# Attention in fp32: sums of values in 64-row by 32-column tiles over two halves of the keys, with a new order of the matmuls

## The chip, the cores and the metric

One Trainium2 chip, one core. The metric is the time of one execution on the device in microseconds (us); shorter is better.

## What is computed

Two rounds of the same two layers on x of 2048 rows and 640 columns, all in fp32:

```python
x = x + _A_ref(_layernorm(x), A_wqkv, A_wo)              # attention, 32 heads of 20
x = x + _B_ref(_layernorm(x), B_w1, B_b1, B_w2, B_b2)    # 640 -> 1536, squared relu, -> 640
# and both lines once more

scores = jnp.einsum("bhqd,bhkd->bhqk", q, k) * (Dh ** -0.5)
p = _softmax(scores, axis=-1)
o = jnp.einsum("bhqk,bhkd->bhqd", p, v)
```

## The kernel before

A layer A runs in three stages: the projections to q, k and v (`qkv`), the attention (`attention`), and the product with wo. Then comes layer B. The change lies in `attention`.

**Blocks and tiles.** Four heads form a group, and 512 queries of a group form a block `t`; there are 32 blocks. A block goes through the 2048 keys in 16 tiles of 128 keys, so a layer has 512 key tiles. For one key tile TensorE does three things:

- *Scores* (`score`, line 565): four matmuls, one for each head, with keys as rows of the result. q and k are laid out so that a head uses 62 rows of the array: two heads (letter `a` in the order below) lie on rows 0 to 63, the other two (`b`) on rows 64 to 127. A score on the lower half of the rows can so run beside one on the upper half. ScalarE takes the exponential of each result (line 572) and writes it to a tile `e`.
- *Sums of values* (`pv`, line 577): four matmuls, one for each head, which multiply `e` by the values (with a column of ones, for the sum of the weights) and add to one bank over the 16 key tiles of the block. Each uses all 128 rows and 32 columns of the array. The letter `V` stands for the four. They are plain fp32, and each shows as two passes in the trace.
- *Maxima* for a later block (`smax`, line 481, letters `m` on the lower half of the rows and `n` on the upper): the softmax needs the largest score of each query beforehand, so scores are computed a second time with queries as rows, and VectorE reduces each result to its maximum (line 493). A part of this work was done already in `qkv`. 

**PSUM banks.** The scores go through banks 0 to 3 in turn (`ps_st`), the maxima through banks 4, 5 and 6 (`sm_ring`), and the sums of values of a block collect in bank 7. When a block's 16 tiles are through, `finish` copies bank 7 out on VectorE (line 590), and small steps on POOL and SyncE's DMA queue divide by the sum of the weights.

**Order.** Nothing is scheduled automatically here: instructions stand on each engine in the order in which the program makes them. In `attention` this order is written by hand in the strings `ORDERS`. Each string covers 8 key tiles, and its key is the number of pairs of maxima in it. `pairs()` chooses among them by how many maxima are still due; it chooses 12 nearly all the time. TensorE takes its instructions in this order, and one that has to wait for a bank holds back those behind it. The last 16 key tiles of a layer run in another way (`both_heads`, line 1091, two scores for one exponential at line 1098), and have no maxima left.

Of the kernel before, what the change touches and what calls it, by code (L numbers as in the profile page):

```python
# [25 lines left out]
NQB = S // QB  # L26
NG = H // 4
NKT = S // P
# [11 lines left out]
def tile_layers(  # L40
# [11 lines left out]
    nc = tc.nc  # L52
# [10 lines left out]
    def name(p):  # L63
        n_alloc[0] += 1
        return f"{p}{n_alloc[0]}"

    def slot(shape, dtype, label):
        return arena.tile(shape, dtype, tag="slot", name=name(label))

    def dma(eng, dst, src):  # L70

        if dst.dtype == F32R:
            dst = dst.bitcast(F32)
        if src.dtype == F32R:
            src = src.bitcast(F32)
        eng.dma_start(dst, src)
# [4 lines left out]
    banks = psum.tile([P, 8, 512], F32, tag="banks", name="banks")  # L81
# [172 lines left out]
    def split_to(dst_hi, dst_lo, src):  # L254

        nc.scalar.copy(dst_hi, src)
        nc.vector.tensor_sub(dst_lo, src, dst_hi.bitcast(F32))  # L257
# [12 lines left out]
    def pool_hi(dst, src):  # L270
        nc.gpsimd.tensor_copy(dst, src)  # L271
# [3 lines left out]
    def pool_lo(dst, a, b):  # L275
        m = nc.gpsimd.tensor_sub(dst, a, b)
        if last_row:
            after(m, last_row.pop(), "VectorE and Pool share a port")
# [144 lines left out]
    k_t, q_t, v_t, mx_t, kept = {}, {}, {}, {}, {}  # L423
    left, done, split = {}, set(), {}
# [26 lines left out]
    def load_q(t):  # L451
        g, qb = divmod(t, NQB)
        q_t[t] = slot([P, 2, QB], F32R, "q")
        rows_of_heads(q_t[t], d_qk[0, qb], g)
# [34 lines left out]
    def smax(ring, t, p, sub, c, par):  # L489

        dst = ring("sm")
        by_queries(dst, t, p, sub, c, par)
        nc.vector.tensor_reduce(  # L493
            maxima(t)[:, 2 * par + p, sub, c : c + 1], dst, axis=AX.X, op=ALU.max
        )
# [75 lines left out]
        )  # L571
        nc.scalar.activation(es[p][:, par, :], dst, AF.Exp, scale=SCALE)  # L572

    def pv(acc, t, kt, es, heads=(3, 2, 1, 0)):
        for h in heads:
            p, par = divmod(h, 2)
            nc.tensor.matmul(  # L577
                acc[32 * h : 32 * h + 32, :],
                v_t[t // NQB, kt // 8][:, kt % 8, 32 * h : 32 * h + 32],
                es[p][:, par, :],  # L580
                start=(kt == 0),
                stop=(kt == NKT - 1),
            )

    def finish(t, acc):


        g, qb = divmod(t, NQB)
        o = slot([P, 2, QB], F32, "o")
        nc.vector.tensor_copy(o[:, 0, :], acc)  # L590
        res = []

        def store(q):
            ot = res.pop().rearrange("p l t -> p (l t)")
            for h in range(4):
                r0 = (4 * g + h) * DH
                dma(q, d_o[r0 : r0 + DH, qb], ot[32 * h : 32 * h + DH])

        if t == NBLK - 1:

            def invert():
                dst = ps_all("rs")
                nc.tensor.matmul(dst, sums_t, o[:, 0, :], start=True, stop=True)
                nc.vector.reciprocal(o[:, 1, :], dst)

            def divide():
                nc.vector.tensor_mul(o[:, 0, :], o[:, 0, :], o[:, 1, :])
                res.append(slot([P, 2, QB], F32R, "ot"))
                split_to(res[0][:, 0, :], res[0][:, 1, :], o[:, 0, :])

            return [invert, divide, lambda: store(nc.scalar)]

        few = small.tile([P, 16], F32, tag="few", bufs=2, name=name("few"))
        for h in range(4):
            dma(nc.sync, d_s[t, h : h + 1], o[32 * h + DH : 32 * h + DH + 1, 0, :])

        def load():
            dma(nc.sync, few, d_s[t].rearrange("h (q j) -> (h q) j", j=16))

        def invert():  # L620
            nc.gpsimd.tensor_tensor(few, few, minus_t, op=ALU.pow)  # L621

        def spread():
            dma(nc.sync, d_r[t].rearrange("h (q j) -> (h q) j", j=16), few)

        def gather():
            for h in range(4):
                dma(nc.sync, o[32 * h : 32 * h + 32, 1, :], d_r[t, h].partition_broadcast(32))

        def divide():  # L630
            ot = slot([P, 2, QB], F32R, "ot")
            nc.gpsimd.tensor_mul(o[:, 0, :], o[:, 0, :], o[:, 1, :])
            pool_hi(ot[:, 0, :], o[:, 0, :])
            pool_lo(ot[:, 1, :], o[:, 0, :], ot[:, 0, :].bitcast(F32))
            res.append(ot)

        return [load, invert, spread, gather, divide, lambda: store(nc.sync)]
# [46 lines left out]
    def qkv(first, x_src, rest, scores):  # L684
# [271 lines left out]


    ORDERS = {
        16: "bananVanmbanmbbmannaVbmnambVbamnmbVm" * 2,
        15: "anbmnanbaabmbnammbnaVbmbmmbVmbananVanmbanVnambmbVanbmnaVnmbaanVmbbanmV",  # L960
        14: "mbbbanmbbmambmVanannaVmbnaaanVbmabnmVanbmbmbVnaanmbVmabmbanVbmannaVn",
        13: "baanmbVmbanambbnbmVanbmnaVnaabnmbVanbmaanVnmbbanaVmnbmabVabbmmnaVm",
        12: "naambbmVanmbambVbmannabVnabnmabVabnmbanVbbmnanaVbmmbaanVbmbmnaaV",
    }

    def attention(first, x_src, first_rows):
        last = NBLK * NKT
        es_of = {}
        e_n.clear()
        weights.extend(slot([P, 2, QB], F32, "e") for _ in range(6))  # L970
        st_n, sm_n = [0, 0], [0, 0]
        state = {"begun": -1, "done": 0, "acc": None, "debt": 0}
        sm_ring = Ring(4, 5, 6)
        todo = [
            (t, p, sub, c)
            for t in range(NBLK)
# [11 lines left out]
        ends = {x[0]: n for n, x in enumerate(todo)}  # L988
# [3 lines left out]
        rows = {"next": min(t for t in range(NBLK) if t not in done), "at": None}  # L992
# [33 lines left out]
        def op(o):  # L1026
            if o in "ab":
                par = "ab".index(o)
                i, p = divmod(st_n[par], 2)
                if i >= last:  # L1030
                    return
                st_n[par] += 1
                if i > state["begun"]:
                    state["begun"] = i
                    begin(i)
                score(i // NKT, i % NKT, 2 * p + par, es_of.setdefault(i, {}))
            elif o in "mn":
                par = "mn".index(o)
                n = sm_n[par]
                if n == len(todo):  # L1040
                    return
                t, p, sub, c = todo[n]
                if n == firsts[t] and par == 0:
                    for s in blocks[blocks.index(t) :][:2]:
                        if s not in q_t:
                            load_q(s)
                if (t // NQB, c) not in k_t or t not in q_t:
                    return
                sm_n[par] += 1
                smax(sm_ring, t, p, sub, c, par)  # L1050
                if n == ends[t] and min(sm_n) > n:
                    over.add(t)
                    if t * NKT > state["begun"] + 2 * NKT:
                        del q_t[t]
            else:
                i = state["done"]
                if i >= last or i < last - NKT and min(st_n) < 2 * (i + 1):
                    return
                t, u = divmod(i, NKT)
                if u == 0:  # L1060
                    state["acc"] = banks[:, 7, :]
                pv(state["acc"], t, u, es_of.pop(i))
                state["done"] += 1
                if u == NKT - 1:
                    steps = finish(t, state["acc"])
                    split.update((i + j, f) for j, f in zip((4, 6, 7, 9, 11, 12), steps))
                t = rows["next"]
                if rows["at"] is not None:
                    if state["begun"] >= rows["at"]:
                        mrows_load(t)  # L1070
                        rows.update(next=t + 1, at=None)
                elif t in over and t in q_t and state["begun"] >= (t - 2) * NKT + 4:
                    mrows_max(t)
                    mrows(t)
                    rows["at"] = state["begun"] + 2
# [26 lines left out]
        def pairs():  # L1102

            n, i = min(sm_n), state["begun"] + 1
            most = max(
                [8 * (e + 1 - n) / max(t * NKT - 3 - i, 1) for t, e in ends.items() if e >= n],
                default=0,
            )
            state["debt"] += most
            n = min(max(int(state["debt"]), 12), 16)  # L1110
            state["debt"] -= n
            return n

        free.extend((5, 6))
        for o in "abab":
            op(o)
# [14 lines left out]
            both_heads(p)  # L1131
        while state["done"] < last:
            op("V")
            for p in (1, 0):
                if state["wide"] < last:
                    both_heads(p)
# [356 lines left out]
```

## Time and profile before

| | |
|---|---|
| median of 2 runs | 3583.48 us (3583.39 to 3583.57) |
| span of the profiled execution, first to last instruction | 3581.5 us |
| what lies around the span (median less span) | 2.0 us |
| busy: TensorE matmuls | 3569.0 us, 100% |
| busy: VectorE | 2753.5 us, 77% |
| busy: ScalarE | 2647.3 us, 74% |
| TensorE's granted clock | full in all slices |

The profiled execution has no time of its own beside its span; the two timed runs stand for it. In the rows, PE is TensorE's matmuls, PEld its weight loads, DVE is VectorE, ACT ScalarE. A matmul's start is shown with its weight load, also where the array takes up the data only once the weights are in; its end is modelled. Attention fills the stretches from about 310 to 1394 us and from about 2090 to 3174 us.

### The profile page before, as it was taken

The page shows a single profiled execution, that of the slowest core. Times are in us where ns is not written, and L with a number is a line of the kernel's source. Part 1 is how long each engine was busy: PE and PEld are TensorE (multiplying, and loading weights), DVE is VectorE, ACT ScalarE, POOL GpSimd, SP SyncE. Part 2 cuts the span into 40 slices and gives each one's busy share as a digit, 9 for nine tenths or more (in the row PEclk, how much of TensorE's full clock was granted, in tenths as well). Part 3 has the DMA queues.
Part 4 walks back from the last instruction along what each step waited for, and adds up shares of the span by engine and source line. Part 5 has one row for each costly group of instructions (what it writes and reads, how often), then busy time and mean ns, then how long its engine had stood idle before and what let it go on. Part 6 is the DMA issues. An engine that isn't in the chain of part 4 may idle for free.

```text
span 3581.5 us, 67667 instructions
## 1 busy us (share of the span) xinstructions
PE 3569.0 (100%) x25560; PEld 2121.6 (59%) x25560; DVE 2753.5 (77%) x5085; ACT 2647.3 (74%) x5146; POOL 805.2 (22%) x880
## 2 busy tenths in 40 slices
PE   9999999999999999999999999999999999999999
PEld 7896343333334335999988954333334433369998
DVE  8778999999999993455567789999999999824443
ACT  3778999999999995122237789999999999942221
POOL 6531434211211211111153201211211211211110
PEclk9999999999999999999999999999999999999999
DMA  9765555323211136834477652232232211367221
GB/s 305 274 230 167 168 157 155 105 69 81 57 44 51 46 95 204 262 99 115 134 275 244 192 149 70 62 81 60 66 79 54 52 39 45 112 216 248 74 80 39
DMA packets 377397, 452.58 MB, mean 126 GB/s; under 512 B 176642, under 2 KB 223746, under 8 KB 377070
## 3 DMA queue, kind: packets, MB, share of 16 engines
q1 hardware_dynamic: 376254, 445.89, 41.6%
q8 instruction: 201, 3.29, 0.4%
q10 hardware_dynamic: 816, 2.36, 0.2%
q14 instruction: 126, 1.03, 0.1%
HBM read 273.83 MB, written 174.30 MB: 125 GB/s over the span
## 4 chain that ended last, share of the span: by engine, by line
PE 96%; DVE 2%; DMA 1%; issue 0%; ACT 0%; POOL 0%; SPq 0%; ACTq 0%; DVEq 0%
PE banks L577 28%; PE banks L565 20%; PE banks L481 16%; PE banks L293 13%; PE banks L331 10%; PE banks L1259 9%; DVE mx L493 1%; PE banks L1091 1%; DMA q<-d_qk 0%; ACT e L1098 0%; DVE bst L244 0%; DVE xnT L257 0%; DVE x L252 0%; DMA d_qk<-ev 0%; PE banks L408 0%
## 5 line engine op out<-in xcount | busy, mean ns | idle before, releaser
L572 ACT ACTIVATE e<-banks 128x512 f32<-128x512 f32 x3968 | 2049.4, 604 | 61.1 <-PE banks L481 1.7
L493 DVE TENSOR_REDUCE mx<-banks 128x1 f32<-128x512 f32 x3076 | 1929.6, 683 | 208.4 <-PE banks L481 137.2
L481 PE MATMUL banks<-k,q 60*128 60x512 f32 x3586 | 1244.3, 427 | 1.0 <-DMA q<-d_qk 0.5
L565 PE MATMUL banks<-q,k 62*128 62x512 f32 x3968 | 1118.7, 434 | 0.4 <-DVE mx L510 0.4
L577 PE MATMUL banks<-e,vg 128*32 128x512 f32 x8192 | 1091.0, 605 | 1.5 <-ACT e L1098 1.5
L565 PEld LDWEIGHTS banks<-q,k 62*128 62x128 f32 x3968 | 584.4, 185 | 657.8 <-ACT e L572 625.6
L481 PEld LDWEIGHTS banks<-k,q 60*128 60x128 f32 x3586 | 582.0, 184 | 283.1 <-DVE mx L493 210.8
L510 DVE CUSTOM_DVE_ANT_0 rl<-banks,rl 128x512 f32<-128x512 f32 x510 | 332.6, 688 | 101.6 <-PE banks L481 91.0
L331 PE MATMUL banks<-xnT,wqk 64*128 64x512 f32 x2400 | 379.7, 394 | 0.3 <-ACT mark_t L333 0.3
L1244 ACT ACTIVATE r<-banks,b_t 128x512 f32<-128x512 f32 x96 | 66.2, 689 | 419.7 <-PE banks L293 418.3
L577 PEld LDWEIGHTS banks<-e,vg 128*32 128x32 f32 x8192 | 161.1, 108 | 360.2 <-issue 333.1
L502 ACT ACTIVATE rl<-banks 128x512 f32<-128x512 f32 x510 | 270.8, 597 | 98.9 <-PE banks L481 93.6
L1259 PE MATMUL banks<-w,h 128*128 128x320 f32 x2304 | 340.4, 309 | 0.0
L1259 PEld LDWEIGHTS banks<-w,h 128*128 128x128 f32 x2304 | 339.2, 188 | 1.2
L293 PE MATMUL banks<-xnT,w 128*128 128x512 f32 x1440 | 329.4, 389 | 0.0
L331 PEld LDWEIGHTS banks<-xnT,wqk 64*128 64x128 f32 x2400 | 286.4, 185 | 34.3 <-issue 2.4
L293 PEld LDWEIGHTS banks<-xnT,w 128*128 128x128 f32 x1440 | 269.6, 188 | 55.3
L271 POOL CAST mr<-nt 128x32 fp32r<-128x32 f32 x64 | 13.4, 209 | 1143.5 <-DVE nt L536 1143.5
L621 POOL TENSOR_TENSOR few<-few,minus_t 128x16 f32<-128x16 f32 x62 | 179.8, 2900 | 215.6 <-DMA few<-d_s 213.7
L331 PE MATMUL banks<-wv,xnT 64*128 64x320 f32 x1920 | 199.2, 307 | 0.9 <-ACT mark_t L333 0.9
L331 PEld LDWEIGHTS banks<-wv,xnT 64*128 64x128 f32 x1920 | 186.5, 185 | 2.7 <-ACT mark_t L333 1.4
L1245 DVE TENSOR_TENSOR r<-r 128x512 f32<-128x512 f32 x96 | 74.3, 774 | 124.0 <-ACT r L1244 124.0
(86 smaller groups left out, 2010.8 us busy)
## 6 DMA issues: line engine op xcount, KB each, us to landing
q<-d_qk SPq DMA_DIRECT2D x242, 240.0 KB
d_qk<-ev SPq DMA_DIRECT2D x80, 512.0 KB
k<-d_qk SPq DMA_DIRECT2D x152, 240.0 KB
x<-d_x SPq DMA_DIRECT2D x84, 320.0 KB
d_qk<-ev SPq DMA_DIRECT2D x80, 256.0 KB
d_o<-ot SPq DMA_DIRECT2D x248, 80.0 KB
ot<-d_o SPq DMA_DIRECT2D x38, 512.0 KB
d_v<-v SPq DMA_DIRECT2D x32, 512.0 KB
```

The costliest lines, as they stand in the source:

```text
L293: nc.tensor.matmul(dst, a, b, start=(n == 0), stop=(n == last))
L331: m = nc.tensor.matmul(ch["dst"][:, :width], *pair, start=first, stop=last)
L481: nc.tensor.matmul(dst, q_t[t][b : b + 60, p, sub * P : (sub + 1) * P], k_t[t // NQB, c][b : b + 60, p, :], start=True, stop=True,)
L493: nc.vector.tensor_reduce(maxima(t)[:, 2 * par + p, sub, c : c + 1], dst, axis=AX.X, op=ALU.max)
L502: nc.scalar.activation(res, dst, AF.Relu)
L510: nc.vector.tensor_tensor_reduce(out=r, in0=dst, in1=r, scale=1.0, scalar=LEAST, op0=ALU.add, op1=ALU.max, accum_out=maxima(t)[:, 2 * par ...
L565: nc.tensor.matmul(dst, k_t[t // NQB, kt // 4][b : b + 62, p, (kt % 4) * P : (kt % 4 + 1) * P], q_t[t][b : b + 62, p, :], start=True, stop ...
L572: nc.scalar.activation(es[p][:, par, :], dst, AF.Exp, scale=SCALE)
L577: nc.tensor.matmul(acc[32 * h : 32 * h + 32, :], v_t[t // NQB, kt // 8][:, kt % 8, 32 * h : 32 * h + 32], es[p][:, par, :], start=(kt == 0 ...
L621: nc.gpsimd.tensor_tensor(few, few, minus_t, op=ALU.pow)
L1245: nc.vector.tensor_mul(r, r, r)
L1259: nc.tensor.matmul(dst[:, :HALF], hs[f][:, hx, i * P : (i + 1) * P], w_2.piece(at_2(f0 + f, hw, hf)), start=(f == 0 and (hx, hw) == THREE[0]),
```

## The change

The sums of values are taken in two halves of the keys: letter `V` is the four matmuls on rows 0 to 63, letter `W` the four on rows 64 to 127. Each is so a tile of 64 rows and 32 columns. `V` adds to bank 7 and `W` to bank 6, and `finish` adds the two. Bank 6 is no longer there for the maxima, which go through banks 4 and 5 alone. The strings of the order are new, and there are three of them instead of five.

```diff
-    def pv(acc, t, kt, es, heads=(3, 2, 1, 0)):
+    def pv(acc, t, kt, es, half, heads=(3, 2, 1, 0)):
+
+        rows = slice(64 * half, 64 * half + 64)
         for h in heads:
             p, par = divmod(h, 2)
             nc.tensor.matmul(
                 acc[32 * h : 32 * h + 32, :],
-                v_t[t // NQB, kt // 8][:, kt % 8, 32 * h : 32 * h + 32],
-                es[p][:, par, :],
+                v_t[t // NQB, kt // 8][rows, kt % 8, 32 * h : 32 * h + 32],
+                es[p][rows, par, :],
...
-    def finish(t, acc):
+    def finish(t, accs):
...
-        nc.vector.tensor_copy(o[:, 0, :], acc)
+        nc.vector.tensor_copy(o[:, 0, :], accs[0])
+        nc.vector.tensor_add(o[:, 0, :], accs[1], o[:, 0, :])
...
     ORDERS = {
-        16: "bananVanmbanmbbmannaVbmnambVbamnmbVm" * 2,
...
-        12: "naambbmVanmbambVbmannabVnabnmabVabnmbanVbbmnanaVbmmbaanVbmbmnaaV",
+        12: "babnambanVWmbanVWm" * 4,
+        14: "amnabmbnVWanbamnbmVW" * 4,
+        16: "amnabmbnVWanbamnbmVW" * 4,
     }
...
-        sm_ring = Ring(4, 5, 6)
+        halves = [0, 0]
+        accs = [banks[:, 7, :], banks[:, 6, :]]
+        sm_ring = Ring(4, 5)
...
-                [8 * (e + 1 - n) / max(t * NKT - 3 - i, 1) for t, e in ends.items() if e >= n],
+                [8 * (e + 1 - n) / max(t * NKT - 5 - i, 1) for t, e in ends.items() if e >= n],
...
-            n = min(max(int(state["debt"]), 12), 16)
-            state["debt"] -= n
+            n = min(max(int(state["debt"]) & ~1, 12), 16)
+            state["debt"] = max(state["debt"] - n, -1)
...
         while state["done"] < last:
             op("V")
+            op("W")
```

On TensorE, in the middle of the second attention, two key tiles stood as follows before. `L481` is a matmul for a maximum, `L565` one for a score, `L577` two of the sums of values; "waits DVE" is a wait for VectorE to have emptied the bank, "waits Activation" one for ScalarE.

```order
L577 MATMUL banks<-e_4744,vg_5877 32x512 x2
L577 MATMUL banks<-e_4743,vg_5877 32x512 x2
L565 MATMUL banks<-q_6209,k_4881 128x512 [waits Activation_49] x2
L481 MATMUL banks<-k_5325,q_6234 128x512 [waits DVE_49] x2
L565 MATMUL banks<-q_6209,k_4881 128x512 [waits Activation_49] x2
L481 MATMUL banks<-k_5325,q_6234 128x512 [waits DVE_49]
L577 MATMUL banks<-e_4746,vg_5877 32x512 x2
L577 MATMUL banks<-e_4745,vg_5877 32x512 x2
```

Each key tile had its four scores and three maxima between two groups of sums. Now, in the same part of the program (`L579` is the line of the sums of values in the changed kernel):

```order
L579 MATMUL banks<-e_4746,vg_6279 32x512 x2
L579 MATMUL banks<-e_4745,vg_6279 32x512 x2
L481 MATMUL banks<-k_5310,q_5955 128x512 [waits DVE_49]
L565 MATMUL banks<-q_5634,k_4992 128x512 [waits Activation_49] x3
L481 MATMUL banks<-k_5310,q_5955 128x512 [waits DVE_49]
L565 MATMUL banks<-q_5634,k_4992 128x512 [waits Activation_49]
L481 MATMUL banks<-k_5310,q_5955 128x512 [waits DVE_49]
L565 MATMUL banks<-q_5634,k_5092 128x512 [waits Activation_49] x2
L481 MATMUL banks<-k_5310,q_5955 128x512 [waits DVE_49]
L579 MATMUL banks<-e_4748,vg_6279 32x512 x2
L579 MATMUL banks<-e_4747,vg_6279 32x512 x2
```

This is a long stretch of six scores and four maxima (`m`, then `babnamban`); behind it come eight matmuls of sums, `V` and `W`, of which the first four are shown. Then follows a short stretch of two scores and two maxima (`mban`), and again `V` and `W`:

```order
L481 MATMUL banks<-k_5310,q_5955 128x512 [waits DVE_49]
L565 MATMUL banks<-q_5634,k_5092 128x512 [waits Activation_49] x2
L481 MATMUL banks<-k_5310,q_5955 128x512 [waits DVE_49]
L579 MATMUL banks<-e_4744,vg_6279 32x512 x2
L579 MATMUL banks<-e_4743,vg_6279 32x512 x2
```

So two key tiles still hold eight scores and six maxima, but they lie 10 and 4, where before they lay 7 and 7. This unit of two key tiles fills 960 of the 1024 key tiles of the two layers; 32 are the last 16 of each layer, 16 run by the string of 14, and the rest stand at the beginnings and ends. On VectorE, at the end of a block, before:

```order
L493 TENSOR_REDUCE mx_5287<-banks 128x1 [waits PE_49] x27
L590 COPY o_5497<-banks 128x512 [waits DMAHW3_49,PE_49]
L493 TENSOR_REDUCE mx_5287<-banks 128x1 [waits PE_49] x12
L525 TENSOR_REDUCE nm_88<-mx_913 128x16
L536 STREAM_TRANSPOSE nt_5588<-nm_88 128x32 [waits DVE_49,Pool_49]
```

And now:

```order
L493 TENSOR_REDUCE mx_5388<-banks 128x1 [waits PE_49] x26
L592 COPY o_5624<-banks 128x512 [waits DMAHW3_49,PE_49]
L593 TENSOR_TENSOR o_5624<-banks,o_5624 128x512 [waits DVE_49,PE_49]
L493 TENSOR_REDUCE mx_5388<-banks 128x1 [waits PE_49] x10
L525 TENSOR_REDUCE nm_88<-mx_913 128x16
L536 STREAM_TRANSPOSE nt_5716<-nm_88 128x32 [waits DVE_49,Pool_49]
```

The addition of the two banks stands behind the copy, ahead of the reductions of the next long stretch. L525 and L536, which prepare the maxima of a block, stand behind ten reductions instead of twelve, which is behind the last reduction of a long stretch.

More of the change, by code (lines that the diff above doesn't have):

```diff
@@ L958, in tile_layers @@
     ORDERS = {
-        16: "bananVanmbanmbbmannaVbmnambVbamnmbVm" * 2,
-        15: "anbmnanbaabmbnammbnaVbmbmmbVmbananVanmbanVnambmbVanbmnaVnmbaanVmbbanmV",
-        14: "mbbbanmbbmambmVanannaVmbnaaanVbmabnmVanbmbmbVnaanmbVmabmbanVbmannaVn",
-        13: "baanmbVmbanambbnbmVanbmnaVnaabnmbVanbmaanVnmbbanaVmnbmabVabbmmnaVm",
-        12: "naambbmVanmbambVbmannabVnabnmabVabnmbanVbbmnanaVbmmbaanVbmbmnaaV",
+        12: "babnambanVWmbanVWm" * 4,
+        14: "amnabmbnVWanbamnbmVW" * 4,
+        16: "amnabmbnVWanbamnbmVW" * 4,
     }
@@ L971, in attention @@
         st_n, sm_n = [0, 0], [0, 0]
-        state = {"begun": -1, "done": 0, "acc": None, "debt": 0}
-        sm_ring = Ring(4, 5, 6)
+        state = {"begun": -1, "done": 0, "debt": 0}
+        halves = [0, 0]
+        accs = [banks[:, 7, :], banks[:, 6, :]]
+        sm_ring = Ring(4, 5)
         todo = [
@@ L1055, in op @@
             else:
-                i = state["done"]
+                half = "VW".index(o)
+                i = halves[half]
                 if i >= last or i < last - NKT and min(st_n) < 2 * (i + 1):
@@ L1059, in op @@
                 t, u = divmod(i, NKT)
-                if u == 0:
-                    state["acc"] = banks[:, 7, :]
-                pv(state["acc"], t, u, es_of.pop(i))
+                pv(accs[half], t, u, es_of[i], half)
+                halves[half] += 1
+                if min(halves) == state["done"]:
+                    return
                 state["done"] += 1
+                es_of.pop(i)
                 if u == NKT - 1:
-                    steps = finish(t, state["acc"])
+                    steps = finish(t, accs)
                     split.update((i + j, f) for j, f in zip((4, 6, 7, 9, 11, 12), steps))
```

## The prediction

> **What bounds the kernel now.** I read the page first, then the groups of instructions in a steady part of the attention, then single rows. The page:
>
> ```profile
> span 3581.5 us, 67667 instructions
> PE 3569.0 (100%) x25560; PEld 2121.6 (59%) x25560; DVE 2753.5 (77%) x5085; ACT 2647.3 (74%) x5146; POOL 805.2 (22%) x880
> ```
>
> TensorE is never idle, but its ends are modelled, so this does not yet say that it sets the pace. The groups and busy times between 500 and 1200 us:
>
> ```profile
> 500.00:1200.00 700.00, 700.00 (x4945) 278.88 (x4943) 637.85 (x1050) 680.89 (x1319) 166.26 (x175) 1.00 0.30 82
> L572 ACT ACTIVATE e<-banks 128x512 f32<-128x512 f32 x1319 | 681.4, 604 | 19.1
> L493 DVE TENSOR_REDUCE mx<-banks 128x1 f32<-128x512 f32 x989 | 620.6, 683 | 60.3 <-PE banks L481 36.4 <-PE banks L565 22.6
> L577 PE MATMUL banks<-e,vg 128*32 128x512 f32 x2640 | 351.6, 605 | 0.0
> L481 PE MATMUL banks<-k,q 60*128 60x512 f32 x988 | 335.4, 431 | 0.0
> ```
>
> A key tile has eight rows on L577 (four heads, two passes), so 2640 rows are 330 key tiles, **2.12 us each**, with 989 / 330 = 3.0 maxima. ScalarE (681 of 700 us) and VectorE (638) are nearly full too. Which of the three sets the pace, single rows tell (start, length, engine, line):
>
> ```profile
> 801.60 1.07 PE L577 MATMUL banks<-e,vg 128*32 128x512 f32 x8
> 802.05 0.61 PE L577 MATMUL banks<-e,vg 128*32 128x512 f32 x4
> 802.59 0.50 PE L565 MATMUL banks<-q,k 62*128 62x512 f32 x1
> 802.60 0.50 PE L481 MATMUL banks<-k,q 60*128 60x512 f32 x1
> 802.93 0.39 PE L565 MATMUL banks<-q,k 62*128 62x512 f32 x1
> 802.94 0.62 PE L481 MATMUL banks<-k,q 60*128 60x512 f32 x2
> 803.17 0.62 PE L565 MATMUL banks<-q,k 62*128 62x512 f32 x2
> 803.72 1.07 PE L577 MATMUL banks<-e,vg 128*32 128x512 f32 x8
> 809.99 1.57 ACT L572 ACTIVATE e<-banks 128x512 f32<-128x512 f32 x3
> ```
>
> From sums to sums: 803.72 - 801.60 = 2.12. The sums take two passes 0.45 apart (802.05 - 801.60), and 0.99 until the first score. Scores and maxima go in pairs, one on each half of the rows: the second pair 0.34 after the first, later ones 0.23 apart (803.17 after 802.94). Seven matmuls make four on one half: 0.34 + 2 x 0.23 = 0.80 from first to last; then 0.32 to the next sums, which closes the period (0.99 + 0.80 + 0.32 = 2.11). No wait is left in it: **TensorE sets the pace.** ScalarE could go faster: three exponentials back to back take 1.57, the last 0.61, so one every 0.48, or 1.92 for a key tile.
>
> Two costs are in these steps beyond the streaming. A pair takes 0.23, yet 0.32 pass before the sums; and the second pass starts at 802.05, so should be through by 802.50 as the first was after 0.45, yet the first scores load at 802.59 and stream another 0.11 later (0.34 against 0.23). So each change between 64x128 and 128x32 tiles costs about 0.1 of emptying, and exposes the weight load.
>
> **The change, part by part.** *1. Sums in eight tiles.* Is the emptying still there when the tiles are 64 rows high on both sides? No row shows 64x128 against 64x32. The nearest is the end of the attention, where 128x32 sums are followed by the 128x128 product with wo, so that only the columns change:
>
> ```profile
> 1393.25 1.06 PE L577 MATMUL banks<-e,vg 128*32 128x512 f32 x8 [0.74 <-ACT e L1098]
> 1394.24 0.56 PE L293 MATMUL banks<-wo,ot 128*128 128x320 f32 x2
> ```
>
> 0.99 again, the same as where rows and columns both change. I take it that a change of columns alone empties the array, so a group of sums keeps its 0.99 + 0.32. The Trainium skill says so more widely: "TensorEngine Tiling (Array Packing)", Key Properties, has it that any change of the tiling mode, as against another tile of the same mode, drains TensorE. By that rule V and W drain as before and the sum is the one below; without it the third or fourth rival holds.
>
> `V` and `W` lie on different rows and add to different banks. The four tiles of a group run at once now (eight passes of 0.6 in 1.07), and so do a score and a maximum on the two halves (802.59 and 802.60), so I let the eight run at once. The four more starts cost about 0.03 (estimate: the modelled 1.07 holds two passes 0.45 apart and 0.61 long, which leaves about 0.01 for three starts). So 1.02 for `V W`; bounds 0.99 and, if they do not overlap at all, twice that.
>
> *2. The balance of the halves.* Two key tiles now have 10 and 4 matmuls, so 5 and 2 pairs instead of 4 and 4. If nothing waited: 1.03 + 0.34 + 2 x (0.32 + 1.02) = 4.05, or 2.03 for a key tile, 0.09 less than now.
>
> *3. Two banks for maxima.* How long does one use of a bank take?
>
> ```profile
> 808.97 0.29 PEld L481 LDWEIGHTS banks<-k,q 60*128 60x128 f32 x2
> 809.53 0.69 DVE L493 TENSOR_REDUCE mx<-banks 128x1 f32<-128x512 f32 x1 [0.25 <-PE banks L481]
> 551.82 1.94 DVE L493 TENSOR_REDUCE mx<-banks 128x1 f32<-128x512 f32 x3
> 552.55 0.18 PEld L481 LDWEIGHTS banks<-k,q 60*128 60x128 f32 x1
> 552.72 0.39 PE L481 MATMUL banks<-k,q 60*128 60x512 f32 x1
> ```
>
> An idle VectorE begins its reduction 0.56 after the weight load (0.45 after streaming begins). The load at 552.55 waits for the reduction begun at 551.82: 0.73 from a reduction's start to the next use of its bank. That is **1.29 for one use of a bank**. Reductions back to back come every 0.60 to 0.63 (three in 1.94, the last 0.69); I take 0.60. With two banks, the third maximum of a stretch waits for the first, and the fourth for the second. Everything behind a waiting matmul waits too, since TensorE's order is fixed: the scores behind it, the sums, and so ScalarE.
>
> Worked through, with T = 0 at the first weight load of a long stretch, M1 to M4 its maxima, M5 and M6 those of the short one:
> - M1 loads at 0; reduction at 0.56; its bank is free at 1.29.
> - M2 comes third on its half, streams at 0.57 and has data at 1.02, but VectorE is busy until 1.16; bank free at 1.16 + 0.73 = 1.89.
> - M3 could stream at 0.80. It loads at 1.29; reduction at 1.85.
> - M4 loads at 1.89 and streams at 2.00, instead of 1.03 without waits; reduction at 2.45, bank free at 3.18. **The stretch is 0.97 longer.**
> - `V W` load at 2.00 + 0.32 = 2.32 and last until 3.34. VectorE runs dry at 3.05.
> - Short stretch: M5 loads at 3.34 (its bank is free since 1.85 + 0.73 = 2.58), M6 streams at 3.68 (free since 3.18). M5's reduction is at 3.90, M6's at 4.50. No wait.
> - `V W` load at 4.00, until **5.02**. Then M1's bank is free since 4.63, M2's from 5.23, before 5.02 + 0.57.
>
> So 2.51 for a key tile against 2.12: +0.39 x 960 = **+374 us**. ScalarE needs 8 x 0.48 = 3.84 of the 5.02 and VectorE 6 x 0.60 = 3.60, so neither binds. The bounds: 2.03 if no bank is waited for; about 2.57 if `V W` take 0.06 more.
>
> *4. Copy and addition at a block's end.*
>
> ```profile
> 821.97 0.68 DVE L590 COPY o<-banks 128x512 f32<-128x512 f32 x1
> 822.57 3.73 DVE L493 TENSOR_REDUCE mx<-banks 128x1 f32<-128x512 f32 x6
> 826.53 1.89 DVE L493 TENSOR_REDUCE mx<-banks 128x1 f32<-128x512 f32 x3 [0.24 <-PE banks L481]
> L257 DVE TENSOR_TENSOR xnT<-banks,xnT 128x512 fp32r<-128x512 f32 x20 | 12.8, 679 | 5.9 <-ACT xnT L256 5.9
> ```
>
> Now VectorE makes up for the copy by dropping its pauses of a quarter of a microsecond (six reductions in a row), at no cost to TensorE. The addition is priced by a subtraction with one operand in a bank: 0.68 long, 0.60 to 0.68 for what is behind it. Copy and addition begin when `W` ends, at about T = 0.1, so M1's reduction starts at about 1.4 instead of 0.56, and M2, M3, M4 move with it: +0.84, bounds 0 and 0.84. No pause covers it there, as the two banks wait for this very reduction. 60 blocks x 0.84 = +50 us. L525 and L536 (0.21 each) fall into VectorE's pause between 3.05 and 3.90. The sums of the next block come long after the addition.
>
> *5. The rest.* The string of 14 (16 key tiles) has four maxima in each stretch, so each key tile costs about 2.32 + 1.02 = 3.34: +1.2 x 16 = +20 us; some of it comes back as key tiles without maxima, so bounds 0 and 20. The last 16 key tiles of a layer are ScalarE's:
>
> ```profile
> L1098 ACT ACTIVATE e<-banks 128x1024 f32<-128x1024 f32 x24 | 22.2, 1239 | 0.0
> L577 PE MATMUL banks<-e,vg 128*32 128x512 f32 x88 | 11.7, 605 | 0.0
> ```
>
> Eleven key tiles in these 20 us, 1.82 each, with two exponentials of 22.2 / 24 = 0.93. TensorE needs 0.99 + 0.34 + 0.32 = 1.65 of it, so 0.03 more is hidden; without that cover it would be 1 us in all. The DMAs of `finish` are the same and leave about 0.7 later, with steps spread over several key tiles.
>
> Sum: 3581.5 of the profiled execution + 374 + 50 + 20 = 4025.5, and with the 2.0 between span and median about **4027**; I say 4025.
>
> **The rivals.** *First, it works as meant* (2.03): the waits for banks are hidden and the better balance shows: 3583 - 0.09 x 960 = 3497, faster. It needs a bank's use to be under 0.69 (M1 to M3 without waits), about half of the 1.29 in the rows. 5%.
>
> *Second, `W` runs behind `V`.* `pv` issues head by head, two passes for each. Were passes started strictly in this order, the sums would now take five steps of 0.45; they take 0.99, so a later head passes an earlier one. Still, `W`'s first passes could stand behind `V`'s second: +0.45 in each of 976 key tiles, 4025 + 439 = 4464. In the Trainium skill, "TensorE: Matmul & The Clock Gate", Part 3, matmuls keep strict program order in start and end; by that rule this rival holds, and the trace speaks against the rule. 5%.
>
> *Third, no emptying, but the weight loads stay exposed.* Each half goes on by itself. The upper half's round is then b, b, M2 (0.46), M4 a bank's use later (1.75), `W` at 1.98 for 0.88 (0.45 for its first pass, a little less for its last), b, M6, `W` again: 1.98 + 0.88 + 0.46 + 0.88 = 4.20, and 2 x 0.14 for loads: 4.48, or 2.24. +0.12 x 960 + 50 + 20 = 3768. 14%.
>
> *Fourth, not slower: neither emptying nor exposed loads.* The same round without the 0.28 is 2.10 for a key tile; -0.02 x 960 + 50 + 20 = 3634, +1.4%. The bank's use then just eats what the missing emptying gives. It decides if a score on the lower half starts while `W` still runs on the upper. The two identical 0.99 speak against it. 8%.
>
> **How the numbers follow.** The forecast has 68%. Its own range is 3930 to 4110 (`V W` 0.06 longer: +58; steps 4 and 5 at zero: -70). The range is 3700 to 4120: with the third rival, without the first, second and fourth (18%). 2% is about what a measurement of this kernel can tell from no change. Faster by over 2%: the first, 0.05. Within 2%: the fourth, 0.08. Slower: 68 + 5 + 14 = 0.87.
>
> **What would show it.** Groups of sums alternately about 1.7 and 3.3 us apart, so 5.0 for two; 0.32 and 1.02 around `V W`; two waits of L481's load for VectorE in each long stretch; VectorE and ScalarE at about 75 and 80% in the attention. If eight passes take much over 1.1, or scores start under a running `W`, step 1 is wrong; if L481 does not wait, step 3 is.

## Result and profile after

| | before | after |
|---|---|---|
| time, median of 2 runs | 3583.48 us | 4037.36 us (4036.27 to 4038.45) |
| ratio, with 95% interval | | 1.127 [1.125, 1.129] |
| span of the profiled execution | 3581.5 us | 4034.5 us |
| VectorE busy | 77% | 71% |
| ScalarE busy | 74% | 66% |

The change makes the kernel 12.7% slower; 4025 was forecast. The head of the page of the changed kernel, the shares of its chain by engine, and the clock of its 40 slices:

```profile
span 4034.5 us, 84165 instructions
PE 3803.3 (94%) x33752; PEld 2125.6 (53%) x33752; DVE 2850.5 (71%) x5149; ACT 2653.9 (66%) x5146; POOL 804.7 (20%) x880
...
PEclk9999999999999999999999999999999999999999
...
PE 84%; DVE 13%; issue 1%; DMA 1%; ACT 1%; POOL 0%; SPq 0%; DVEq 0%; ACTq 0%; POOLq 0%
```

TensorE has 8192 rows more (33752 against 25560: the sums in eight tiles) and yet, for the first time, idle time. VectorE, which has hardly more work than before, now stands on 13% of the chain. The groups between 500 and 1200 us (busy and mean duration, then idle time before them and what ended it), with the busy times of the stretch (PE, PEld, DVE, ACT, POOL, and the granted clock) ahead of them, and two rows of its waits (total, times, longest) behind:

```profile
500.00:1200.00 700.00, 638.80 (x6184) 229.56 (x6178) 550.16 (x881) 556.27 (x1073) 148.81 (x162) 1.00 0.27 77
```

```profile
L493 DVE TENSOR_REDUCE mx<-banks 128x1 f32<-128x512 f32 x813 | 522.9, 686 | 146.1 <-PE banks L565 108.6 <-PE banks L481 37.4
L481 PE MATMUL banks<-k,q 60*128 60x512 f32 x813 | 356.1, 464 | 61.0 <-DVE mx L493 60.7
L579 PE MATMUL banks<-e,vg 64*32 64x512 f32 x4296 | 294.6, 605 | 0.0
```

```profile
PEld banks L481 <- DVE mx L493: 335.8, 407, 1.8
PEld banks L565 <- ACT e L572: 33.6, 123, 0.8
```

A key tile has sixteen rows of sums now: 4296 / 16 = 268.5 key tiles in the 700 us, 2.61 us each against 2.12. Matmuls of L481 wait 60.7 us for VectorE to empty a bank, and the weight loads of L481 335.8, while VectorE itself is idle for 146.1 us before L493, waiting for TensorE's results. Two engines that wait for each other in turn, neither of them full: this is how too few buffers look. (Of the loads' waits, two in each unit of two key tiles cost nothing: they lie under the sums, the 0.84 in the rows below.) The weight loads of one unit, and its matmuls:

```profile
799.51 0.18 PEld L481 LDWEIGHTS banks<-k,q 60*128 60x128 f32 x1 [0.84 <-DVE mx L493]
...
800.79 0.18 PEld L481 LDWEIGHTS banks<-k,q 60*128 60x128 f32 x1 [0.75 <-DVE mx L493]
801.22 0.18 PEld L565 LDWEIGHTS banks<-q,k 62*128 62x128 f32 x1 [0.17 <-ACT e L572]
801.39 0.18 PEld L481 LDWEIGHTS banks<-k,q 60*128 60x128 f32 x1
...
802.84 0.18 PEld L481 LDWEIGHTS banks<-k,q 60*128 60x128 f32 x1 [0.84 <-DVE mx L493]
```

```profile
799.51 0.50 PE L481 MATMUL banks<-k,q 60*128 60x512 f32 x1
799.52 0.73 PE L565 MATMUL banks<-q,k 62*128 62x512 f32 x3
800.08 0.39 PE L481 MATMUL banks<-k,q 60*128 60x512 f32 x1
800.79 0.49 PE L481 MATMUL banks<-k,q 60*128 60x512 f32 x1 [0.31 <-DVE mx L493]
801.39 0.50 PE L481 MATMUL banks<-k,q 60*128 60x512 f32 x1
801.82 1.09 PE L579 MATMUL banks<-e,vg 64*32 64x512 f32 x16
802.84 0.50 PE L481 MATMUL banks<-k,q 60*128 60x512 f32 x1
803.19 0.40 PE L481 MATMUL banks<-k,q 60*128 60x512 f32 x1
803.51 1.09 PE L579 MATMUL banks<-e,vg 64*32 64x512 f32 x16
804.53 0.50 PE L481 MATMUL banks<-k,q 60*128 60x512 f32 x1
```

With T = 0 at 799.51, the six maxima stand at 0, 0.57, 1.28, 1.88, 3.33 and 3.68, the two groups of sums at 2.31 and 4.00, and the next unit begins at 5.02. The table of the forecast had 0, 0.57, 1.29, 1.89, 3.34 and 3.68, 2.32 and 4.00, 5.02. The third maximum waits 0.75; the fourth shows no wait of its own, since a score ahead of it waits 0.17 for ScalarE (801.22). At the end of a block, VectorE:

```profile
844.42 1.29 DVE L493 TENSOR_REDUCE mx<-banks 128x1 f32<-128x512 f32 x2 [0.76 <-PE banks L565]
845.68 0.69 DVE L592 COPY o<-banks 128x512 f32<-128x512 f32 x1
846.48 0.69 DVE L593 TENSOR_TENSOR o<-banks,o 128x512 f32<-128x512 f32 x1
847.09 2.56 DVE L493 TENSOR_REDUCE mx<-banks 128x1 f32<-128x512 f32 x4
```

and on TensorE the first and the third maximum of the stretch behind it, the third 0.73 after the reduction's start at 847.09:

```profile
845.57 0.50 PE L481 MATMUL banks<-k,q 60*128 60x512 f32 x1
...
847.82 0.50 PE L481 MATMUL banks<-k,q 60*128 60x512 f32 x1 [1.28 <-DVE mx L493]
```

### The profile page after: what moved, and what is told of

It is laid out like the page before. It is cut to its first block, busy times and chain, and to the rows that moved or that the text cites. A ratio compares the mean times of both kernels' runs of the same rounds, so it can differ in the third digit from the quotient of the medians.

```text
span 4034.5 us, 84165 instructions
## 1 busy us (share of the span) xinstructions
PE 3803.3 (94%) x33752; PEld 2125.6 (53%) x33752; DVE 2850.5 (71%) x5149; ACT 2653.9 (66%) x5146; POOL 804.7 (20%) x880
## 4 chain that ended last, share of the span: by engine, by line
PE 84%; DVE 13%; issue 1%; DMA 1%; ACT 1%; POOL 0%; SPq 0%; DVEq 0%; ACTq 0%; POOLq 0%
PE banks L579 24%; PE banks L481 22%; PE banks L293 12%; DVE mx L493 10%; PE banks L331 9%; PE banks L1266 8%; PE banks L565 8%; DVE o L593 1%; DVE o L592 1%; DMA q<-d_qk 0%; PE banks L1097 0%; DVE bst L244 0%; ACT e L1104 0%; SPq L76 0%; ACT e L572 0%
## 5 line engine op out<-in xcount | busy, mean ns | idle before, releaser
L493 DVE TENSOR_REDUCE mx<-banks 128x1 f32<-128x512 f32 x3076 | 1976.3, 686 | 550.3 <-PE banks L565 389.6
L481 PE MATMUL banks<-k,q 60*128 60x512 f32 x3586 | 1531.5, 454 | 216.8 <-DVE mx L493 214.3
L481 PEld LDWEIGHTS banks<-k,q 60*128 60x128 f32 x3586 | 622.5, 184 | 1307.2 <-DVE mx L493 1218.6
L565 PE MATMUL banks<-q,k 62*128 62x512 f32 x3968 | 1277.9, 443 | 3.2 <-ACT e L572 2.8
L579 PE MATMUL banks<-e,vg 64*32 64x512 f32 x16384 | 1120.4, 603 | 1.4 <-ACT e L1104 1.4
L565 PEld LDWEIGHTS banks<-q,k 62*128 62x128 f32 x3968 | 560.5, 185 | 130.9 <-ACT e L572 127.8
L579 PEld LDWEIGHTS banks<-e,vg 64*32 64x32 f32 x16384 | 186.1, 105 | 314.5 <-issue 309.1
L293 PE MATMUL banks<-xnT,w 128*128 128x512 f32 x1440 | 329.4, 389 | 0.0
```

Source lines behind the costliest of these rows:

```text
L293: nc.tensor.matmul(dst, a, b, start=(n == 0), stop=(n == last))
L481: nc.tensor.matmul(dst, q_t[t][b : b + 60, p, sub * P : (sub + 1) * P], k_t[t // NQB, c][b : b + 60, p, :], start=True, stop=True,)
L493: nc.vector.tensor_reduce(maxima(t)[:, 2 * par + p, sub, c : c + 1], dst, axis=AX.X, op=ALU.max)
L565: nc.tensor.matmul(dst, k_t[t // NQB, kt // 4][b : b + 62, p, (kt % 4) * P : (kt % 4 + 1) * P], q_t[t][b : b + 62, p, :], start=True, stop ...
L579: nc.tensor.matmul(acc[32 * h : 32 * h + 32, :], v_t[t // NQB, kt // 8][rows, kt % 8, 32 * h : 32 * h + 32], es[p][rows, par, :], start=(k ...
```

## Experiments

The theory to be tried, which held only in part (the table behind experiment 4): the change costs what it does because two banks do not carry the maxima; the new order and the split of the sums matter little beside that. One rival is that the new order costs the time (10 and 4 matmuls, where ScalarE or VectorE run dry); the other that the split sums do (more starts, or `W` behind `V`). In the diffs, "before" and "after" say from which kernel an experiment departs; "time" is the median, and ratios are to the kernel before (3583.3 to 3584.0 in these comparisons).

**1. Two banks alone** (from before).

```diff
-        sm_ring = Ring(4, 5, 6)
+        sm_ring = Ring(4, 5)
```

> The kernel before with one thing changed: the maxima go through two banks (4, 5) instead of three; sums and order stay. My theory (the third maximum of a stretch waits 1.29 us for the first one's bank): in the old order each key tile has three maxima, so each waits about 0.6, and what stands behind it too: 2.7 to 2.9 us for a key tile instead of 2.12, about 4160 to 4300 us. Rival A (the uneven order of 10 and 4 matmuls is what costs, two banks are enough): 3583. Rival B (the 64-row tiles cost it): 3583.

Time 4332.15 us, 1.209 [1.206, 1.213]: a little above the range given. Rows of its groups between 500 and 1200 us:

```profile
L481 PE MATMUL banks<-k,q 60*128 60x512 f32 x727 | 301.9, 458 | 105.7 <-DVE mx L493 102.2
...
L577 PE MATMUL banks<-e,vg 128*32 128x512 f32 x1936 | 257.8, 605 | 0.0
```

1936 / 8 = 242 key tiles, 2.89 us each, with 102.2 us of idle TensorE before L481 that VectorE ends. Sums and order are untouched here, so the loss of the bank is enough by itself. In the old order it costs more than the whole change does.

**2. The new order alone** (from before: the new strings without `W`, and the two lines that choose among them; three banks for maxima).

```diff
-        12: "naambbmVanmbambVbmannabVnabnmabVabnmbanVbbmnanaVbmmbaanVbmbmnaaV",
+        12: "babnambanVmbanVmbabnambanVmbanVmbabnambanVmbanVmbabnambanVmbanVm",
...
+            n = min(max(int(state["debt"]) & ~1, 12), 16)
```

> The kernel before with the new order alone: 10 and 4 matmuls between the sums, sums still of 128 rows in one bank, three banks for the maxima. If only the banks for maxima matter, M4 alone waits a little (1.40 instead of 1.03): about 2.2 for a key tile, 3660. My theory with the four banks of the scores counted in the same way (the fifth and sixth score of the long stretch wait for the exponentials of the first two, which end 1.18 and 1.65 after the stretch's start): M4 at 1.76, 4.72 for two key tiles, about 3812. Rival A (the order is the whole cost): about 4000. Rival that the better balance shows: about 3500.

Time 3860.62 us, 1.077 [1.074, 1.081]; about 50 more than expected. The order is not free. Between 500 and 1200 us, a row of the groups and two of the waits:

```profile
L577 PE MATMUL banks<-e,vg 128*32 128x512 f32 x2320 | 309.0, 605 | 0.0
```

```profile
PEld banks L481 <- DVE mx L493: 240.3, 289, 0.8
PEld banks L565 <- ACT e L572: 114.5, 290, 0.8
```

2320 / 8 = 290 key tiles, 2.41 us each. The 289 waits of L481, two in a unit, are those under the sums, which cost nothing; three banks are enough for the maxima. But the loads of scores wait for ScalarE twice in a unit, 114.5 / 145 = 0.79 in all:

```profile
801.61 0.18 PEld L565 LDWEIGHTS banks<-q,k 62*128 62x128 f32 x1 [0.46 <-ACT e L572]
802.10 0.18 PEld L565 LDWEIGHTS banks<-q,k 62*128 62x128 f32 x1 [0.31 <-ACT e L572]
```

The fifth and sixth score of a stretch find the four banks of `ps_st` full. Without waits the unit should be 3.99 here (the 4.05 of step 2 of the prediction, less 0.03 for each of two groups of sums that are not split), and 3.99 + 0.77 = 4.76 with them; from the sums of one unit to those of the next the rows have 4.81 (799.39 to 804.20).

**3. The new order with two banks** (experiment 2 and the edit of experiment 1; sums as before). What is then left to the changed kernel is the split sums alone.

> The kernel before with the new order and two banks for the maxima, but the sums as they were (128 rows, one bank, no addition). It differs from the changed kernel only in the sums, so it prices the new tiles alone. My theory: 0.03 for each of about 976 key tiles and 54 us for the additions (the run without them) less than the changed kernel: about 3954. If the 64-row tiles save emptying: 4037 or more. If they cost more than I think: under 3930.

Time 3960.64 us, 1.105 [1.102, 1.109], as expected. With two banks the new order is so 371 us faster than the old (4332.15), with three 277 us slower. The changed kernel's time less this one is 77 us: the price of the split sums. Against experiment 2 the loss of the third bank costs only 100 us here (3960.64 less 3860.62).

**4. The split sums and two banks in the old order** (from after).

```diff
-        12: "babnambanVWmbanVWm" * 4,
+        12: "naambbmVWanmbambVWbmannabVWnabnmabVWabnmbanVWbbmnanaVWbmmbaanVWbmbmnaaVW",
```

> The changed kernel with the old strings, V written as VW: two accumulators, 64-row tiles, two banks for maxima, seven matmuls in each stretch. My theory: as the kernel before with two banks, and 0.03 for the eight tiles and about 50 us for the additions: 4240 to 4380, slower than with the new order. Rival A (the uneven order is the cost): back to about 3600 to 3660. Rival B (the 64-row tiles are the cost): about 4000.

In this kernel and in the second one of experiment 7, the string of 14, which runs 8 key tiles of a layer, lets the scores run so far ahead that two heads' exponentials of a key tile are written over before they are summed; the sums of these key tiles are not the right ones, but the instructions are the same. Time 4420.3 us, 1.234 [1.230, 1.237], above the range again. Against experiment 1 it is 88 us, so the split sums cost much the same here as in the new order (77). Order and banks by themselves, and with the split sums below them, in us:

| | old order | new order |
|---|---|---|
| three banks for maxima | 3583 (before) | 3861 |
| two banks for maxima | 4332 | 3961 |
| two banks and split sums | 4420 | 4037 (the change) |

The bank costs 749 in the old order and 100 in the new one; the new order costs 277 with three banks and wins 371 with two. So the 454 us of the change cannot be shared out between bank and order without saying which comes first: order 277, bank 100, split sums 77, or bank 749, order -371, split sums 77. The loss of the bank is enough by itself for a loss of time, but the rival of the order is not refuted: with three banks, the new order alone makes more than half of the loss. The rival of the split sums is: 77 or 88 of the time.

**5. Half of each maximum reduced** (from after). It shortens a bank's use, and with it VectorE's work.

```diff
-            maxima(t)[:, 2 * par + p, sub, c : c + 1], dst, axis=AX.X, op=ALU.max
+            maxima(t)[:, 2 * par + p, sub, c : c + 1], dst[:, :256], axis=AX.X, op=ALU.max
```

> The changed kernel, with the maxima in the attention taken over 256 of each 512 columns (so the maxima are not the true ones): the matmuls stay, VectorE's reduction is about half as long. My theory: a bank comes free about 0.27 sooner, M4 streams at about 1.58 instead of 2.00 if only these banks bind (3835); with the score banks counted, at 1.76: about 3920. If the wait does not come from the reduction holding the bank: 4037.

Time 3920.3 us, 1.094 [1.091, 1.097], as expected. The groups between 500 and 1200 us:

```profile
L493 DVE TENSOR_REDUCE mx<-banks 128x1 f32<-128x256 f32 x854 | 345.7, 422 | 311.8 <-PE banks L481 149.5 <-PE banks L565 142.5
L481 PE MATMUL banks<-k,q 60*128 60x512 f32 x855 | 369.6, 463 | 25.5 <-DVE mx L493 19.4
```

A reduction of 422 ns instead of 686 takes the idle time before L481 from 61.0 to 25.5 us and the time down by 117 us, although VectorE was idle for a fifth of the stretch before: what counts is when a bank comes free, not the engine's mean busy share. It does not go back to 3583. The order's own wait for banks of scores is left: 3920 is near what the new order with three banks (3861) and the split sums (77) come to, 3938, and the last score of a long stretch waits 0.31 for ScalarE (its load at 800.37), as in experiment 2.

**6. Without the addition at a block's end** (from after).

```diff
-        nc.vector.tensor_add(o[:, 0, :], accs[1], o[:, 0, :])
```

> The changed kernel without the addition of the second accumulator at a block's end (the upper half of the keys is left out of the sums). The trace of the changed kernel has 5.01 for a usual unit and 6.00 where a block ends. My theory: the reduction of M1 starts 0.6 to 0.68 sooner there, and the whole unit is that much shorter: 60 blocks, 36 to 41 us, about 3998. If the addition is covered: 4037.

Time 3982.94 us, 1.112 [1.110, 1.114]: 54 us less than the changed kernel, 0.91 for each of the 60 blocks, and 15 below the 3998 expected. The rows give a little less for the addition. From the sums ahead of a usual long stretch to those behind it the changed kernel takes 3.33 (798.49 to 801.82), and where a block ends 4.29 (844.55 to 848.84); without the addition it takes 3.33 (798.26 to 801.59) and 3.50 (793.09 to 796.59). So the addition is 0.79 of the 0.96, 47 us in 60 blocks, and the copy 0.17; of the other 7 us some can be the halved clock, of which the changed kernel has more. Of the 77 of experiment 3, the addition is the larger part; the rest, some 22 to 30 us over 976 key tiles, is 0.02 to 0.03 for a group of eight tiles instead of four.

**7. Three banks for scores and three for maxima**, with the sums as before (from before; its diff is shown) and with the split sums (from after, with the strings of experiment 4 and the same banks).

```diff
-    ps_st = Ring(0, 1, 2, 3)
+    ps_st = Ring(0, 1, 2)
...
-        sm_ring = Ring(4, 5, 6)
+        sm_ring = Ring(3, 4, 5)
```

> The kernel before with three banks for scores and three for maxima (bank 6 unused), old order and old sums: the companion of the next run. My theory: the fourth score of each stretch waits for the first one's exponential, so about 2.6 for a key tile, around 4030.

> The changed kernel with the old strings (V as VW) and three banks for scores and three for maxima: it differs from its companion only in the sums (eight 64-row tiles, two accumulators, one addition for a block). My theory: the sums cost 0.03 for a key tile and the additions at most 50 us: 30 to 80 us over the companion. If the emptying is less with 64-row tiles: under the companion. If V and W do not run at once: over 400 us more.

Times 4069.10 us, 1.135 [1.133, 1.138], and 4097.32 us, 1.143 [1.141, 1.146]; the first is a little above the 4030 expected, the second 28 us above the first, just below the 30 to 80 expected. With three banks for the maxima the split sums so cost 28, with two 77 or 88: most of the price of the addition comes with the missing bank. The row of the score loads in the first:

```profile
L565 PEld LDWEIGHTS banks<-q,k 62*128 62x128 f32 x1072 | 162.2, 184 | 334.1 <-ACT e L572 329.4
```

The wait only moves, from VectorE's banks to ScalarE's (329.4 us). The eighth bank is missing on whichever side it is taken from. None of the runs that gives a bank away comes near the kernel before; the changed kernel's order is the best of those tried that split the sums and leave nothing out.

**8. `V` and `W` apart** (from after). A score on the upper half (`b`) stands between them. `V` lies on the lower half; behind `W`, on the upper, comes a maximum on the lower half (`m`). If a change of tiles empties only its own half, or does not empty the array at all, this is nearly free.

```diff
-        12: "babnambanVWmbanVWm" * 4,
+        12: "babnamanVbWmbanVWm" * 4,
```

> The changed kernel with one upper-half score moved between V and W of the long stretch (babnamanVbWmbanVWm): the same work. If a change of tiles empties the whole array, V and W are two groups there, each with its 0.99 and 0.32, so 1.3 us more in each unit of two key tiles: 6.3 instead of 5.0, about 4660. If the halves go on by themselves (no emptying; the third and fourth rival of the prediction), the score runs beside V: 4037 or less.

Time 5554.42 us, 1.550 [1.547, 1.553]: far above the 4660 expected. Two things are mixed in it. Where the clock is full:

```profile
907.62 1.06 PE L579 MATMUL banks<-e,vg 64*32 64x512 f32 x8
908.62 0.49 PE L565 MATMUL banks<-q,k 62*128 62x512 f32 x1
909.04 1.06 PE L579 MATMUL banks<-e,vg 64*32 64x512 f32 x8
910.03 0.50 PE L481 MATMUL banks<-k,q 60*128 60x512 f32 x1
```

`V` takes 1.00 to the score, the score 0.42 to `W`, `W` 0.99 to the next matmul, the maximum. The score goes to the upper half, which nothing occupies, and waits until `V` on the lower is through; the maximum goes to the lower half and waits until `W` on the upper is through. (The 0.42 tells nothing of the halves, since the score and `W` are on the same one.) So the whole array is emptied, as step 1 assumed, also between 64x128 and 64x32. By the Trainium skill, "TensorEngine Tiling (Array Packing)", Key Properties, any change of tiling mode drains TensorE; the 1.00 before the score and the 0.99 before the maximum agree. A unit at full clock takes 6.40 (907.62 to 914.02), near the 6.3 worked out ahead of the run, which would make about 4700 us (an estimate: 4037 and 480 units, each 1.38 over the 5.02). The other thing is the clock (page and windows of the same kernel; the PEclk row counts in tenths, the number behind the busy times is the mean granted clock):

```profile
PE   9999999999999999999999999999999999999999
...
PEclk9996777777776676699999777866667877677999
```

```profile
500.00:1200.00 700.00, 676.07 (x3889) 203.26 (x3881) 348.29 (x550) 359.71 (x677) 121.11 (x142) 0.73 0.23 67
```

TensorE's clock falls to half again and again in the attention, and with it goes the rest of the time, some 850 us.

**9. Only the lower half of the sums** (from after, without the matmuls of `W`; the addition takes the bank of `V` twice). Less work, in the same order with the same banks; it was to show what `W` costs beside `V`.

```diff
-        for h in heads:
+        for h in () if half else heads:
...
-        nc.vector.tensor_add(o[:, 0, :], accs[1], o[:, 0, :])
+        nc.vector.tensor_add(o[:, 0, :], accs[0], o[:, 0, :])
```

> The changed kernel without W's matmuls (the upper half of each key tile is left out of the sums; the addition takes the first bank twice, so VectorE does the same). Two questions. Does W cost anything beside V? My theory: 0.03 for a key tile, so about 4008 at full clock. And the granted clock: in the run with the sums apart it fell to 0.81 of full, with V and W each filling half of the rows at a time. If it falls because half of the rows stand idle in the sums, it falls here too, and the time goes up by hundreds of microseconds; if it fell there for another reason, it stays at 1.00.

Time 5464.19 us, 1.525 [1.502, 1.548], 1427 us more than the changed kernel with 8192 rows fewer on TensorE. Its clock (page), and sums at full and at half clock:

```profile
PEclk9996555555555555599999655555555555555999
```

```profile
350.12 1.06 PE L579 MATMUL banks<-e,vg 64*32 64x512 f32 x8
351.11 0.50 PE L481 MATMUL banks<-k,q 60*128 60x512 f32 x1
...
1001.13 1.93 PE L579 MATMUL banks<-e,vg 64*32 64x512 f32 x8
1002.99 0.79 PE L481 MATMUL banks<-k,q 60*128 60x512 f32 x1
```

At full clock `V` alone takes 0.99 to the next matmul (350.12 to 351.11) where `V W` take 1.02: `W` beside `V` costs 0.03, and they run at once. The clock falls, the first of the two outcomes named ahead of the run. As a measure of the whole time the run is of no use, since the clock decides it.

## Why the prediction came out right, step by step

*Step 1* held. `V W` take 1.02, and the stretches keep 0.99 and 0.32 to 0.33 around them (803.19 to 803.51). The second rival (`W` behind `V`) needed about 1.45 there. The prediction took the overlap of the passes to speak against a strict program order of the matmuls; the rows do not name the matmul of a pass, so they show only that the first passes of a group run ahead of the second ones, not in which order whole matmuls end. The third and fourth rivals needed an array that one half can leave by itself, which experiment 8 excludes.

*Step 3* came out in its size. 5.02 for a unit is 2.51 for a key tile, (2.51 - 2.12) x 960 = 374 us of the 453.9 by which the median rose. The waits stand at the third and fourth maximum of a long stretch, as worked out. Taking the bank alone brings a loss (experiment 1), and holding the banks a shorter time brings part of it back (experiment 5).

But the prediction put the whole 374 down to the missing bank, with 2.03 for a key tile if no bank is waited for, and here it left something out. In the same order with three banks a unit already takes 4.81 (experiment 2), since the long stretch runs out of banks for scores; the missing bank adds only 100 us in this order (experiment 3 less experiment 2). The prediction asked whether ScalarE has time enough (3.84 of the 5.02, so it does not bind), but not how long the fifth and sixth score wait for one of four banks. The sum is right all the same because the wait that was counted is the longer of the two: the fourth maximum loads 1.88 behind the first here, and 1.71 behind it in experiment 2 (802.10 less 800.39). That the maxima alone gave the right sum is luck.

One more thing in this step is off: two waits of L481 were to be seen in each long stretch, and there is one. The fourth maximum stands where it was put (1.88), and its bank comes free then (the second reduction begins at 800.66, and 800.66 + 0.73 = 801.39); but the load ahead of it, a score's, ends at the same time (801.22 + 0.18), so either of the two would hold it there. Behind a block's end it does wait for VectorE, 0.30 at 848.42.

*Step 4* is the term that was mis-sized: 0.84 for a block's end was worked out, and a unit with a block's end takes 6.00 against 5.01, so +0.99, 59 us instead of 50. The first reduction begins at 847.09, 1.52 behind the stretch's first maximum (845.57) and not at 1.4. Copy and addition were priced as two operations back to back. But the addition reads what the copy writes, and begins 0.80 behind it (845.68 to 846.48), 0.11 after the copy's end, where an independent reduction begins 0.60 to 0.68 behind. By the rows of experiment 6, some 0.8 go with the addition and 0.17 with the copy.

*Step 5*: some 20 us remain (453.9 - 374 - 59 = 21), against 20 for the string of 14 with everything else at nothing. This remainder also holds some 7 us of a halved clock (below), so the 20 is not shown apart.

*VectorE and ScalarE*: 550.16 and 556.27 of 700 us, 79 and 79%, where 75 and 80% were given.

*The first rival*, 3497, asked only for maxima that do not wait, and was priced too well. In experiment 2 they do not, and a key tile is at 2.41, not 2.03, since the four banks of the scores take over as the limit. The 4.05 for a unit without waits agrees to 0.05 with the rows of that experiment (4.81 less the 0.77 of waits, against 3.99 with the sums not split), but this order does not reach it with four banks for scores. So even with the bank's use at nothing the order would have been slower.

The agreement of the unit to 0.01 is partly luck of the case: all its terms (0.56, 0.73, 0.60, 0.99, 0.32) could be read from rows of the kernel before, and only the missing bank was new.

## What to carry to other kernels

Before taking a buffer from a ring, take from the rows how long one use of it lasts, from the producer's start to the next producer's start (here 1.29 us), and lay the uses of one stretch out in order, for every ring that the stretch goes through (here the four banks for scores too, which the prediction left out); the busy shares of the engines do not show the loss, as VectorE and ScalarE stand at 79% in the attention while it happens, below their shares before. An order that gathers work into long stretches needs buffers for the longest stretch, not for the mean. And an operation added at a block's end costs in full (here 0.79 for one that lasts 0.69) where a ring of two waits for the engine that it is put on, although that engine has idle time elsewhere.

## What was unexpected of the hardware

The granted clock of TensorE follows more than whether TensorE is busy. In experiments 8 and 9, its rows fill 97 and 99% of the span, and the clock falls to half in the attention, with means of 0.81 and 0.65 over the span. The runs whose sums use all 128 rows (before, and experiments 1, 2, 3 and the first of 7) have a mean of 0.999 to 1.000. Experiment 1 is among them, although TensorE idles more there than in any other run with a full clock. Where `V` and `W` run side by side the mean is 0.994 to 1.000; in the changed kernel four stretches of 3.4 us each are at half clock, about 7 us lost. In experiment 9, half the array's rows stand idle in each group of sums; in experiment 8, in two of the three groups of a unit. That fits a clock that goes by how much of the array works, but no run varied this share by itself, so it is not shown. In the Trainium skill, "TensorE: Matmul & The Clock Gate", Part 1, the clock is either full or half, by how busy TensorE was in a window of about 3.4 us; the two values and the 3.4 us agree with the trace. That rows at 99% busy do not keep the clock full is not what one would read from it, and here the measurement decides.

At a block's end, the addition, which reads what the copy wrote, starts 0.11 us after the copy's end, and the reduction behind it, which needs neither, 0.08 before the addition's end. That the dependence makes the difference is read from this one place; no run varied it.
